# The start of a gated FNet and SwiGLU kernel: a hand-written order, a split first load, and a shorter warming on a constant

## The chip, the cores and the metric

The kernel runs on one core of a Trainium2 chip. The metric is the device time of one execution in microseconds (us). Besides the times of plain runs there is one profiled execution, whose trace gives the start and duration of every instruction.

The core's engines are named as in the profile: PE (TensorE matmuls), PEld (TensorE's weight loads, which overlap matmuls), DVE (VectorE), ACT (ScalarE), POOL (GpSimd) and SP (SyncE, which issues most DMAs). Each engine works through its own list of instructions in the order in which the program holds them, and waits on semaphores for what other engines and DMAs deliver.

## The reference

```python
x = A_x                                                  # 2048 x 512
g = sigmoid((x * gate_w).sum(-1, keepdims=True))
a = Cr @ (x @ Dr.T) - Ci @ (x @ Di.T)                    # DFT over hidden (512) and sequence (2048)
b = (silu(x @ w1) * (x @ w3)) @ w2                       # w1, w3: 512 x 1376, w2: 1376 x 512
return g * a + (1 - g) * b
```

## The kernel before

All matmuls run on float32 data in the fp32r format. Each operand is split into a high part (`high`, L107, an ACT copy that rounds to fp32r) and a low part (`low`, L110, DVE subtracts the high part from the source), and each product takes three matmuls: high by high, high by low, low by high (`mm3`, L117). In every instruction of this kind the weights are a 128 x 128 tile and the moving operand is 128 x 512.

On top of that, every product of two matrices of 2 x 2 blocks is computed with seven block products instead of eight. The operands of these products are the blocks themselves and sums of them. For x, in `OPS` (L202), the forms are B11, B21, B22 and the sums T1 to T4, with T1 = B12 - B11, T2 = B22 - T1, T3 = B22 - B12 and T4 = B21 - T2 (`SUMS`, `sum_xo`). For a chunk of the weights, the forms are three plain blocks (`WA`) and four sums (`WU`, split into `WB`).

The work has two stages.

- **gate and up** (to about 217 us). Items n = (chunk of 128 columns of w1 and w3, half of the sequence) are worked off by `gate_up(n)`. An item consists of products X (`first1`: WA block 0 by B11), Y (`first2`: WA block 1 by B21), and five more in banks X and Z: with T2, T3, T1 (weights from WB), T4 (from WA) and B22 (from WB). Each product of an item is six matmuls, and 42 make an item. `gate_up(n)` also issues X and Y of item n + 3 (`LOOK` = 3) and prepares the weights for the next item. The loads of weights (`load_w`, one 512 KB transfer for a chunk w, to the tile `ws`) and of x (`load_xo`, four blocks of 512 KB, to the tiles `xs_B`) are issued on SP; results (`store_h`) and prepared weights (`low_wb`) are stored by POOL.
- **the DFT and w2 products** (tile P, the rest of the time). The change does not touch them.

Item 0 is different: its T sums are not there yet, so `plain` computes it with eight block products, into four PSUM banks C00, C01, C10 and C11. `half(i, j, ...)` issues six matmuls into one of them. Chunk 0's block A21 and x's block B12, which only item 0 needs as they are, are split into two borrowed tiles, `a21` and `b12`.

The first lines of the program load the first 128 KB of chunk 0 and x's B11, fill a tile `warm` with zeros on DVE, and run eleven bf16 matmuls on it (`WARM`, L398), which have no part in the result. Then come the other loads, then the preparation of the first operands and the products of item 0, X and Y of items 1 to 3, the T sums, and the prepared weights of chunks 1 to 4.

What is not visible in the lines is the order in which the engines run this start. Up to L674 the program is ordered by a planner, which interleaves the instructions of the start on each engine as it estimates them to become ready. In the trace, matmuls of X1 stand between those of item 0, for example. At L674 `tc.manual_schedule()` is entered, and from there on each engine runs its instructions in the order in which the program's lines issue them. `gate_up` has hooks for such work: functions put into `early`, `mid` and `at_end` for item n are called at these points of `gate_up(n)`.

PSUM has eight banks. Item 0 uses banks 0, 4, 6 and 7; X of item n is in bank n % 4, Y in 4 + n % 2, Z in 6 + n % 2. A bank is written again only when its last reader is done.

Of the kernel before, what the change touches and what calls it, by code (L numbers as in the profile page):

```python
# [12 lines left out]
P = 128  # L13
# [8 lines left out]
NG = NST // 2  # L22
NC = (F + P - 1) // P
NP2 = (NC + 1) // 2
WARM = 11
LOOK = 3
K = 9
W2_AT = (9, 11, 13, 15)
# [4 lines left out]
def fnet_swiglu_gate_kernel(  # L33
# [46 lines left out]
    def bank(k, name):  # L80
        return psum.tile([P, 512], F32, tag=f"ps{k}", name=name)
# [31 lines left out]
    def split(hi, lo, src):  # L113
        high(hi, src)
        low(hi, lo, src)
# [89 lines left out]
    def sum_xo(g, k, t):  # L205
        ST[g, k] = t
        nc.vector.tensor_sub(t, *(ST[g, v] for v in SUMS[k]))
# [5 lines left out]
    def split_xo(g, k):  # L213
        split(*xo_parts(g, k))
# [21 lines left out]
    def prep_wa(w, lo=0, hi=3):  # L236

        if lo == 0:
            WA[w] = wap.tile([P, 2, 3, 256], F32R, tag="wa", name=f"wa{w}")
        split(*wa_parts(w, lo, hi))  # L240
# [24 lines left out]
    def prep_wb(w):  # L265
        sums_wb(w)
        high_wb(w)
        low_wb(w)
# [10 lines left out]
    G = {}  # L279

    def first1(n):
        x = bank(n % 4, f"X{n}")
        prod(x, n, 0, 0, True)
        s1 = s1p.tile([P, 512], F32, tag="s1", name=f"s1_{n}")
        nc.scalar.activation(s1, x, AF.Copy)
        G[n] = (x, s1)

    def first2(n):

        y = bank(4 + n % 2, f"Y{n}")  # L290
        prod(y, n, 1, 1, True)
        s1 = G[n][1]
        nc.vector.tensor_add(s1, s1, y)
        put_score(n, 0, s1)
# [28 lines left out]

    early, mid, at_end = {}, {}, {}

    def run(work, n):
        for f in work.get(n, ()):
# [2 lines left out]
    def gate_up(n):  # L332
        last = NI - 1
        x, s1 = G.pop(n)
        z = bank(6 + n % 2, f"Z{n}")
        if n == last - 1:

            u2, g1 = (s1p.tile([P, 512], F32, tag="s1", name=f"{k}_{n}") for k in ("u2", "g1"))
        else:
            h = hp.tile([P, 1024], F32, tag="h", name=f"h{n}")  # L340
            u2, g1 = h[:, :512], h[:, 512:]
        u4 = u4p.tile([P, 512], F32, tag="u4", name=f"u4_{n}")
        nw = WSET[n + 1] if n < last else 0
# [23 lines left out]
        nc.vector.tensor_add(u4, u4, x)  # L367
        if nw is not None:
            low_wb(nw)
        run(mid, n)  # L370
        prod(z, n, 2, 6, False, True)
        nc.vector.tensor_add(u2, u2, z)
        nc.vector.tensor_mul(u2, s1, u2)  # L373
        store_h(n, 0, u2)
        if wa is not None:
            WA[wa] = wap.tile([P, 2, 3, 256], F32R, tag="wa", name=f"wa{wa}")
# [18 lines left out]
    nc.vector.memset(warm, 0.0)  # L395
    wps = bank(7, "wps")
    for n in range(WARM):
        nc.tensor.matmul(wps, warm[:, :P], warm, start=True, stop=True)  # L398
    nc.scalar.activation(act0, warm[:, :24], AF.Silu)

    def plain(b12, a21):

        c = {}

        def half(i, j, w, x, start):
            if start:
                c[i, j] = bank((0, 4, 6, 7)[2 * i + j], f"C{i}{j}")
            for r in range(2):
                sl = slice(r * P, (r + 1) * P)
                mm3(c[i, j], w(0, sl), w(1, sl), x(r, 0), x(r, 1), start and r == 0,  # L410
                    not start and r == 1)

        def wa(k):
            return lambda h, sl: WA[0][:, h, k, sl]

        def xb(k):
            return lambda q, h: XO[0][:, h, k, q, :]

        w21 = lambda h, sl: a21[:, h, sl]
        x12 = lambda q, h: b12[:, h, q * 512 : (q + 1) * 512]  # L420
        s1 = s1p.tile([P, 512], F32, tag="s1", name="s1_0")
        g1 = u4p.tile([P, 512], F32, tag="u4", name="g1_0")
        h = hp.tile([P, 1024], F32, tag="h", name="h0")
        yield half(0, 0, wa(0), xb(0), True)
        yield half(1, 0, w21, xb(0), True)
        half(0, 0, wa(1), xb(1), False)
        nc.scalar.activation(s1, c[0, 0], AF.Silu)
        yield half(1, 0, wa(2), xb(1), False)
        nc.vector.tensor_mul(h[:, :512], s1, c[1, 0])
        store_h(0, 0, h[:, :512])  # L430
        half(0, 1, wa(0), x12, True)
        yield half(1, 1, w21, x12, True)
        half(0, 1, wa(1), xb(2), False)
        nc.scalar.activation(g1, c[0, 1], AF.Silu)
        half(1, 1, wa(2), xb(2), False)
        nc.vector.tensor_mul(h[:, 512:], g1, c[1, 1])
        yield store_h(0, 1, h[:, 512:])
# [11 lines left out]
    step = plain(b12, a21)  # L449
    prep_wa(0, 0, 1)  # L450
    for q in range(2):
        split(XO[0][:, 0, 0, q], XO[0][:, 1, 0, q], ST[0, "B11"][:, q * 512 : (q + 1) * 512])
    next(step)
    split(a21[:, 0], a21[:, 1], WS[0][:, 3])
    next(step)
    prep_wa(0, 1, 3)
    split_xo(0, "B21")
    next(step)
    split(b12[:, 0], b12[:, 1], ST[0, "B12"])
    next(step)  # L460
    split_xo(0, "B22")
    next(step)
    free(*zt)
    WS.pop(0)
    load_w(4)
    prep_wa(1)
    first1(1)
    first2(1)
    gate1(1)
    sum_xo(0, "T1", hp.tile([P, 1024], F32, tag="h", name="t1"))  # L470
    sum_xo(0, "T2", ST[0, "B11"])
    prep_wa(2)
    first1(2)
    first2(2)
    gate1(2)
    split_xo(0, "T2")
    prep_wb(1)
    sum_xo(0, "T3", ST[0, "B12"])
    split_xo(0, "T3")
    prep_wa(3)  # L480
    first1(3)
    first2(3)
    gate1(3)
    split_xo(0, "T1")
    prep_wa(4)
    sum_xo(0, "T4", ST[0, "B21"])
    split_xo(0, "T4")
    free(*(ST[0, b] for b in ("B11", "B21", "B12", "B22")))
# [506 lines left out]
```

## Time and profile before

| | us |
|---|---|
| median of 3 runs | 711.27 |
| lowest and highest run | 711.21, 711.48 |
| profiled execution, its own time | 710.88 |
| its span, first to last instruction | 709.1 |
| PE busy | 703.9 (99%), 3089 matmuls |
| DVE busy | 604.6 (85%) |
| ACT busy | 369.6 (52%) |
| POOL busy | 64.0 (9%) |

The span leaves out what lies before the first and after the last instruction, 1.8 us here. In a timeline, a row shows the start, the time to the end of the last instruction that is merged into it, the engine, the line, the operation, the tiles written and read (out<-in), the shape, the count, and in brackets how long the engine was idle ahead of it and what ended that. The tile names that matter here: `wps` is the warming matmuls' bank, `C` item 0's banks, `X`, `Y`, `Z` those of the items, `xo` the split forms of x, `wa` and `wb` the split weights, `wu` the weight sums, `ws` and `xs_B` the raw loads, and `a` and `b` the borrowed tiles for A21 and B12. A matmul's row ends 0.39 us after its start while the next one starts 0.23 us after it: matmuls are pipelined, so the distance of starts is what counts.

### The profile page before, as it was taken

To read this page: it belongs to the slowest core of one execution; us is meant where nothing else is said; L and a number is where in the kernel's file an instruction comes from. 1 tells how busy PE (TensorE), PEld (TensorE's weight loads), DVE (VectorE), ACT (ScalarE), POOL (GpSimd) and SP (SyncE) were. 2 spreads that over 40 slices of the span, in tenths; PEclk is the share of its full clock that TensorE was granted. 3 is DMA by queue.
4 is the path that set the end of the run, shared out by engine and by line. 5 is a ranking of instruction groups with operands and counts; after the bars stand their busy time and mean duration, and the time that the engine had idled before them with its cause. 6 is when DMAs were issued, how large, how long until landed. Compare 5 with 4: busy or idle time off the path is not lost.

```text
span 709.1 us, 8589 instructions
## 1 busy us (share of the span) xinstructions
PE 703.9 (99%) x3089; PEld 579.1 (82%) x3089; DVE 604.6 (85%) x733; ACT 369.6 (52%) x478; POOL 64.0 (9%) x118
## 2 busy tenths in 40 slices
PE   9999999999999999999999999999999999999997
PEld 6888888888888888888888888888888888888886
DVE  6979988787679999887999599969997896898985
ACT  6665555655446754454554553544455455455451
POOL 0011111121110000000110001100110000000000
PEclk9999999999999999999999999999999999999999
DMA  7575546589997556712596238814999971773932
GB/s 281 196 295 215 211 188 253 186 313 359 413 412 271 220 207 232 288 60 89 175 358 254 90 122 322 342 48 190 382 419 416 354 270 58 296 285 135 323 119 89
DMA packets 45403, 172.54 MB, mean 243 GB/s; under 512 B 5296, under 2 KB 5424, under 8 KB 41520
## 3 DMA queue, kind: packets, MB, share of 16 engines
q1 hardware_dynamic: 32464, 118.50, 45.2%
q0 software_dynamic: 12608, 52.97, 18.9%
q8 instruction: 24, 0.39, 0.2%
q10 hardware_dynamic: 288, 0.52, 0.2%
q14 instruction: 19, 0.16, 0.1%
HBM read 114.82 MB, written 57.16 MB: 243 GB/s over the span
## 4 chain that ended last, share of the span: by engine, by line
PE 99%; DMA 1%; DVE 0%; ACT 0%; SPq 0%; issue 0%
PE P L119 69%; PE X L119 16%; PE Z L119 8%; PE Y L119 4%; PE C L119 2%; DMA xs_B<-xt 1%; DVE xo L111 0%; DVE zc L788 0%; ACT xo L108 0%; SPq L224 0%
## 5 line engine op out<-in xcount | busy, mean ns | idle before, releaser
L119 PE MATMUL P<-zo,a 128*128 128x512 f32 x1344 | 305.5, 390 | 0.0
L119 PEld LDWEIGHTS P<-zo,a 128*128 128x128 f32 x1344 | 252.1, 188 | 53.2 <-DVE zo L111 1.2
L108 ACT ACTIVATE zo<-B 128x1024 fp32r<-128x1024 f32 (+1 forms) x182 | 189.3, 1045 | 184.5 <-PE P L119 93.2
L111 DVE TENSOR_TENSOR zo<-B,zo 128x1024 fp32r<-128x1024 f32 (+1 forms) x182 | 217.9, 1204 | 48.2 <-ACT zo L108 47.4
L119 PE MATMUL P<-zo,H 128*128 128x512 f32 x468 | 106.2, 389 | 0.0
L119 PEld LDWEIGHTS P<-zo,H 128*128 128x128 f32 x468 | 87.9, 188 | 18.2
L645 DVE TENSOR_TENSOR B<-B,B 128x1024 f32<-128x1024 f32 (+1 forms) x78 | 93.0, 1192 | 0.1
L119 PE MATMUL X<-xo,wb 128*128 128x512 f32 x378 | 92.7, 390 | 0.0
L119 PEld LDWEIGHTS X<-xo,wb 128*128 128x128 f32 x378 | 71.0, 188 | 14.7
L119 PE MATMUL P<-zo,Y 128*128 128x512 f32 x336 | 76.3, 390 | 0.0
L119 PEld LDWEIGHTS P<-zo,Y 128*128 128x128 f32 x336 | 63.1, 188 | 13.1
L322 POOL DMA_DIRECT2D hsp<-h x42 | 23.0, 547 | 126.5 <-DVE h L373 75.6
L119 PE MATMUL X<-xo,wa 128*128 128x512 f32 x126 | 32.3, 390 | 0.0
L119 PE MATMUL Z<-xo,wa 128*128 128x512 f32 x126 | 32.3, 391 | 0.0
L119 PE MATMUL Y<-xo,wa 128*128 128x512 f32 x126 | 32.1, 390 | 0.0
L119 PE MATMUL Z<-xo,wb 128*128 128x512 f32 x126 | 32.1, 390 | 0.0
L648 DVE TENSOR_TENSOR B<-B,B 128x1024 f32<-128x1024 f32 x26 | 31.7, 1219 | 0.0
L863 ACT ACTIVATE zu<-P 128x512 f32<-128x512 f32 x32 | 19.1, 598 | 20.4 <-PE P L119 20.3
L367 DVE TENSOR_TENSOR u<-u,X 128x512 f32<-128x512 f32 x21 | 14.4, 687 | 17.7 <-PE X L119 15.5
L119 PEld LDWEIGHTS Z<-xo,wa 128*128 128x128 f32 x126 | 23.6, 188 | 5.3 <-DVE xo L111 0.4
L119 PEld LDWEIGHTS Y<-xo,wa 128*128 128x128 f32 x126 | 23.7, 188 | 4.9
L119 PEld LDWEIGHTS X<-xo,wa 128*128 128x128 f32 x126 | 23.7, 188 | 4.9
(134 smaller groups left out, 551.3 us busy)
## 6 DMA issues: line engine op xcount, KB each, us to landing
B<-cc SPq DMA_DIRECT2D x64, 512.0 KB, 6.1
hsp<-h POOLq DMA_DIRECT2D x42, 256.0 KB, 3.6
B<-hsp SPq DMA_DIRECT2D x20, 512.0 KB, 9.9
wbsp<-wb POOLq DMA_DIRECT2D x8, 1024.0 KB, 4.3
wb<-wbsp SPq DMA_DIRECT2D x8, 1024.0 KB, 7.8
B<-zsp SPq DMA_DIRECT2D x16, 512.0 KB, 8.4
H<-w2sp SPq DMA_DIRECT2D x6, 1024.0 KB, 9.0
ws<-w SPq DMA_DIRECT2D x11, 512.0 KB, 6.1
```

The source lines that it names most:

```text
L108: nc.scalar.activation(hi, src, AF.Copy)
L111: nc.vector.tensor_sub(lo, src, hi.bitcast(F32))
L119: nc.tensor.matmul(ps, u, v, start=first and n == 0, stop=last and n == 2, skip_group_check=chain)
L322: nc.gpsimd.dma_start(hsp[g, b + k, j // 2, :, j % 2 * 512 : (j % 2 + 1) * 512], h)
L367: nc.vector.tensor_add(u4, u4, x)
L645: nc.vector.tensor_add(t, t, RAW[blk, b, q][:, :n])
L648: nc.vector.tensor_sub(t, RAW[blk, "B12", q], t)
L863: nc.scalar.activation(U[name][:, r], ps[r], AF.Copy)
```

## The change

- `tc.manual_schedule()` is entered before the first load instead of at L674, so the whole start runs in the order written.
- That order is new. After A11 B11 of item 0 come X1, then A21 B11 of item 0, then X2; B21 is used after these. The weights of chunks 1 and 2 are split in two steps, block A11 first. C00 to C11 are then finished, and Y1, Y2, X3 and Y3 follow.
- The loads are reordered and cut: chunks 1 and 2 are loaded in two transfers, the first 128 KB (A11) ahead of the rest, and B11 of x in two transfers of 512 columns.
- In item 0 (`half`) the three matmuls are ordered high by high, low weight by high x, high weight by low x. The other products keep their order.
- The warming reads a constant of ones that the program holds anyway, instead of the tile that DVE filled, and has nine matmuls.
- The sum T4, the low part of T1, the split of T4 and the sum of X and Y of item 2 and 3 move from the start into hooks of `gate_up(1)`; `second` is a new hook after the copy of the Z bank.

```diff
-WARM = 11
+WARM = 9
...
-        nc.sync.dma_start(ST[g, k], xt[g, XRAW.index(k)])
+        n = 512 if not g and k == "B11" else 1024
+        for i in range(0, 1024, n):
+            nc.sync.dma_start(ST[g, k][:, i : i + n], xt[g, XRAW.index(k), :, i : i + n])
...
     def first1(n):
+        copy_x(n, prod1(n))
+
+    def prod1(n):
         x = bank(n % 4, f"X{n}")
         prod(x, n, 0, 0, True)
+        return x
...
         nc.scalar.activation(u4, z, AF.Copy)
+        run(second, n)
...
+    ctx.enter_context(tc.manual_schedule())
     load_w(0, 0, 1)
     load_xo(0, "B11")
-    warm = s1p.tile([P, 1024], mybir.dt.bfloat16, tag="s1", name="warm")[:, :512]
-    nc.vector.memset(warm, 0.0)
+    warm = nc.const_aps.tensor(1.0, [P, 512], mybir.dt.bfloat16)
...
+    load_w(1, 0, 1)
     load_w(0, 1, 4)
+    load_w(2, 0, 1)
     load_xo(0, "B21")
     load_xo(0, "B12")
-    load_w(1)
+    load_w(1, 1, 4)
     load_xo(0, "B22")
-    load_w(2)
+    load_w(2, 1, 4)
     load_w(3)
...
+            for n, (u, v) in enumerate(((0, 0), (1, 0), (0, 1))):
+                nc.tensor.matmul(C[i, j], wp(u, sl), xp(r, v), start=start and r == n == 0,
+                                 stop=not start and r == 1 and n == 2)
...
+    split(*wa_parts(0, 0, 1))
     for q in range(2):
         split(XO[0][:, 0, 0, q], XO[0][:, 1, 0, q], ST[0, "B11"][:, q * 512 : (q + 1) * 512])
+    half(0, 0, 0, 0, True)
+    new_wa(1)
+    split(*wa_parts(1, 0, 1))
+    x1 = prod1(1)
     split(a21[:, 0], a21[:, 1], WS[0][:, 3])
+    half(1, 0, None, 0, True)
+    split(*wa_parts(0, 1, 3))
+    new_wa(2)
+    split(*wa_parts(2, 0, 1))
+    x2 = prod1(2)
     WS.pop(0)
     load_w(4)
+    split_xo(0, "B21")
+    half(0, 0, 1, 1, False)
+    split(b12[:, 0], b12[:, 1], ST[0, "B12"])
+    copy_x(1, x1)
+    half(1, 0, 2, 1, False)
+    split(*wa_parts(1, 1, 3))
+    half(0, 1, 0, None, True)
+    copy_x(2, x2)
+    sums_wb(1)
+    nc.scalar.activation(s1, C[0, 0], AF.Silu)
+    split_xo(0, "B22")
+    half(1, 1, None, None, True)
+    sum_xo(0, "T1", t1)
+    high(*wa_parts(2, 1, 3)[::2])
+    nc.vector.tensor_mul(h0[:, :512], s1, C[1, 0])
+    store_h(0, 0, h0[:, :512])
+    half(0, 1, 1, 2, False)
+    sum_xo(0, "T2", ST[0, "B11"])
+    low(*wa_parts(2, 1, 3))
+    half(1, 1, 2, 2, False)
+    free(*zt)
+    new_wa(3)
+    split(*wa_parts(3, 0, 3))
+    nc.scalar.activation(g1, C[0, 1], AF.Silu)
+    split_xo(0, "T2")
+    y1 = prod2(1)
+    high(*xo_parts(0, "T1")[::2])
+    nc.vector.tensor_mul(h0[:, 512:], g1, C[1, 1])
+    store_h(0, 1, h0[:, 512:])
+    y2 = prod2(2)
+    high_wb(1)
+    sum_g(1, y1)
+    first1(3)
+    sum_xo(0, "T3", ST[0, "B12"])
+    y3 = prod2(3)
+    low_wb(1)
+    split_xo(0, "T3")
     gate1(1)
+    new_wa(4)
+    split(*wa_parts(4, 0, 3))
...
+    do(early, 1, sum_xo, 0, "T4", ST[0, "B21"])
+    do(early, 1, lambda: low(*xo_parts(0, "T1")))
+    do(second, 1, lambda: split_xo(0, "T4"))
+    do(second, 1, free, *(ST[0, b] for b in ("B11", "B21", "B12", "B22")))
+    do(second, 1, sum_g, 2, y2)
+    for n, at, y in ((2, 1, None), (3, 1, y3)):
+        if y is not None:
+            do(mid, at, sum_g, n, y)
+        do(mid, at, gate1, n)
...
-    ctx.enter_context(tc.manual_schedule())
     for n in range(1, NI):
         gate_up(n)
```

More of the change, by code (lines that the diff above doesn't have):

```diff
@@ L234, in wa_parts, with new_wa @@
         return (*(flat(WA[w][:, h, lo:hi]) for h in range(2)), flat(WS[w][:, lo:hi]))
[L236 to L240, printed above, removed]
+    def new_wa(w):
+        WA[w] = wap.tile([P, 2, 3, 256], F32R, tag="wa", name=f"wa{w}")
     WU = {}
@@ L263, in low_wb @@
             nc.gpsimd.dma_start(wbsp[w], WB[w].bitcast(F32))
[L265 to L268, printed above, removed]
     def prod(ps, n, wi, xi, start, chain=False):
@@ L281, in first1, with copy_x @@
     def first1(n):
+        copy_x(n, prod1(n))
+    def prod1(n):
         x = bank(n % 4, f"X{n}")
         prod(x, n, 0, 0, True)
+        return x
+    def copy_x(n, x):
         s1 = s1p.tile([P, 512], F32, tag="s1", name=f"s1_{n}")
@@ L288, in first2, with prod2, sum_g @@
     def first2(n):
+        sum_g(n, prod2(n))
+    def prod2(n):
         y = bank(4 + n % 2, f"Y{n}")
         prod(y, n, 1, 1, True)
+        return y
+    def sum_g(n, y):
         s1 = G[n][1]
@@ L322, in store_h @@
         nc.gpsimd.dma_start(hsp[g, b + k, j // 2, :, j % 2 * 512 : (j % 2 + 1) * 512], h)
-    early, mid, at_end = {}, {}, {}
+    early, second, mid, at_end = {}, {}, {}, {}
     def run(work, n):
@@ L375, in gate_up @@
         if wa is not None:
-            WA[wa] = wap.tile([P, 2, 3, 256], F32R, tag="wa", name=f"wa{wa}")
+            new_wa(wa)
             parts_a = wa_parts(wa, 0, 3)
@@ L399, in fnet_swiglu_gate_kernel @@
     nc.scalar.activation(act0, warm[:, :24], AF.Silu)
[L401 to L437, printed above, removed]
+    load_w(1, 0, 1)
     load_w(0, 1, 4)
+    load_w(2, 0, 1)
     load_xo(0, "B21")
     load_xo(0, "B12")
-    load_w(1)
+    load_w(1, 1, 4)
     load_xo(0, "B22")
-    load_w(2)
+    load_w(2, 1, 4)
     load_w(3)
@@ L448, in fnet_swiglu_gate_kernel, with half @@
     b12, a21 = zt[0].rearrange("p h a n -> p h (a n)"), zt[1][:, :, 0]
-    step = plain(b12, a21)
-    prep_wa(0, 0, 1)
+    C = {(i, j): bank((0, 4, 6, 7)[2 * i + j], f"C{i}{j}") for i in range(2) for j in range(2)}
+    def half(i, j, w, x, start):
+        wp = lambda h, sl: a21[:, h, sl] if w is None else WA[0][:, h, w, sl]
+        xp = lambda q, h: b12[:, h, q * 512 : (q + 1) * 512] if x is None else XO[0][:, h, x, q, :]
+        for r in range(2):
+            sl = slice(r * P, (r + 1) * P)
+            for n, (u, v) in enumerate(((0, 0), (1, 0), (0, 1))):
+                nc.tensor.matmul(C[i, j], wp(u, sl), xp(r, v), start=start and r == n == 0,
+                                 stop=not start and r == 1 and n == 2)
@@ L451, in fnet_swiglu_gate_kernel @@
+    s1 = s1p.tile([P, 512], F32, tag="s1", name="s1_0")
+    g1 = u4p.tile([P, 512], F32, tag="u4", name="g1_0")
+    h0 = hp.tile([P, 1024], F32, tag="h", name="h0")
+    t1 = hp.tile([P, 1024], F32, tag="h", name="t1")
+    new_wa(0)
+    split(*wa_parts(0, 0, 1))
     for q in range(2):
         split(XO[0][:, 0, 0, q], XO[0][:, 1, 0, q], ST[0, "B11"][:, q * 512 : (q + 1) * 512])
-    next(step)
+    half(0, 0, 0, 0, True)
+    new_wa(1)
+    split(*wa_parts(1, 0, 1))
+    x1 = prod1(1)
     split(a21[:, 0], a21[:, 1], WS[0][:, 3])
-    next(step)
@@ L456, in fnet_swiglu_gate_kernel @@
[L456 to L463, printed above, removed]
+    half(1, 0, None, 0, True)
[3 more added lines that the diff above has]
+    x2 = prod1(2)
     WS.pop(0)
     load_w(4)
-    prep_wa(1)
-    first1(1)
-    first2(1)
-    gate1(1)
-    sum_xo(0, "T1", hp.tile([P, 1024], F32, tag="h", name="t1"))
-    sum_xo(0, "T2", ST[0, "B11"])
-    prep_wa(2)
@@ L473, in fnet_swiglu_gate_kernel @@
[L473 to L488, printed above, removed]
+    split_xo(0, "B21")
[3 more added lines that the diff above has]
+    half(1, 0, 2, 1, False)
```

## The prediction

> **What bounds the kernel now.** I read the page first, then PE's waits, then the timelines of PE, ACT and DVE for the first 45 us, because the diff touches nothing that runs later.
>
> The page's head and its chain of waits:
>
> ```profile
> span 709.1 us, 8589 instructions
> ...
> PE 99%; DMA 1%; DVE 0%; ACT 0%; SPq 0%; issue 0%
> PE P L119 69%; PE X L119 16%; PE Z L119 8%; PE Y L119 4%; PE C L119 2%; DMA xs_B<-xt 1%; DVE xo L111 0%; DVE zc L788 0%; ACT xo L108 0%; SPq L224 0%
> ```
>
> The end is set by one stream of matmuls, preceded by the load of the first x block. The change keeps all 3078 real matmuls (3089 less 11 warming ones). Only two things can move the end: when the stream begins, and how often it stops. The timeline of PE (start, us, operation, count):
>
> ```profile
> 1.19 4.67 PE L398 MATMUL wps<-warm 128*128 128x512 bf16 x11 [1.19 <-DVE warm L395]
> 5.62 0.50 PE L119 MATMUL C<-xo,wa 128*128 128x512 f32 x1
> 6.35 1.43 PE L119 MATMUL C<-xo,wa 128*128 128x512 f32 x5 [0.22 <-DVE xo L111]
> 7.62 1.53 PE L119 MATMUL C<-xo,a 128*128 128x512 f32 x6
> 8.98 3.15 PE L119 MATMUL C<-xo,wa 128*128 128x512 f32 x12
> 11.96 1.52 PE L119 MATMUL C<-b,wa 128*128 128x512 f32 x6
> ...
> 31.00 1.83 PE L119 MATMUL Z<-xo,wa 128*128 128x512 f32 x6
> 32.67 1.53 PE L119 MATMUL Y<-xo,wa 128*128 128x512 f32 x6
> ```
>
> A product of six starts 1.36 us after the one before it (7.62 to 8.98), 0.227 a matmul. Against that the stream stops three times: the first six take 2.00 (5.62 to 7.62), 0.64 too many; the twelve from 8.98 take 2.98 instead of 2.72, 0.26 too many (the low part of B21); the Z product takes 1.67, 0.31 too many (T4). Together 1.21. At the later starts of an item (35.39, 44.91, and so on to 73.47) the step is 9.52 for 42 matmuls: nothing is lost.
>
> What feeds the stream, in ACT's timeline and then DVE's:
>
> ```profile
> 4.94 1.15 ACT L108 ACTIVATE xo<-xs_B 128x512 fp32r<-128x512 f32 x2 [1.31 <-DMA xs_B<-xt]
> 7.19 1.06 ACT L108 ACTIVATE xo<-xs_B 128x1024 fp32r<-128x1024 f32 x1 [0.27 <-DMA xs_B<-xt]
> 8.46 1.06 ACT L108 ACTIVATE b<-xs_B 128x1024 fp32r<-128x1024 f32 x1 [0.21 <-DMA xs_B<-xt]
> ```
>
> ```profile
> 8.29 1.23 DVE L111 TENSOR_TENSOR xo<-xs_B,xo 128x1024 fp32r<-128x1024 f32 x1 [0.45 <-ACT xo L108]
> ...
> 30.12 1.23 DVE L111 TENSOR_TENSOR xo<-xs_B,xo 128x1024 fp32r<-128x1024 f32 x1 [0.17 <-ACT xo L108]
> ...
> 33.15 1.23 DVE L111 TENSOR_TENSOR wb<-wu,wb 128x1024 fp32r<-128x1024 f32 x1 [0.53 <-ACT wb L108]
> ...
> 36.22 0.95 DVE L111 TENSOR_TENSOR wa<-ws,wa 128x768 fp32r<-128x768 f32 x1
> ...
> 41.50 0.69 DVE L367 TENSOR_TENSOR u<-u,X 128x512 f32<-128x512 f32 x1 [2.26 <-ACT wb L108]
> ```
>
> Loads land 1.27 us apart per 512 KB. DVE is nearly full from 8.29 until it first has 2.26 to spare, at 41.5. That is the second limit: a PE that starts earlier runs into DVE.
>
> **The start.** The memset (0.27 us on DVE) goes; ACT and SP start work at 0.73, so PE can begin near 0.75. Nine matmuls at the 0.427 pitch of the warming rows end near 4.6, before the data, so the warming itself costs nothing. The first half of B11 is issued at 1.19 as before. Its second half, 256 KB at 1.27 per 512, is 0.64 behind it, so it lands about 4.92 - 0.64 = 4.28 (bounds: 3.69, if it took the 2.5 us of the 128 KB load; 4.92, if it landed with the whole; I take 4.3, because the landings' even spacing carries it). From there ACT needs 0.63 and PE 0.05: first matmul at 4.98 instead of 5.62, a gain of **0.64**. The Trainium skill, "DMA: Bandwidth & Descriptors", anatomy of one DMA, gives about 2.0 us plus bytes over 436 GB/s: that half would land at 3.8, and the start would gain some 0.4 more; the 512 KB row (3.73 where that rule gives 3.2) speaks for the later value.
>
> **The first six.** The new order puts both matmuls that need only high x first, so two run before the low part (DVE 4.96 to 5.64), and the second half lands at 5.0 as the whole did. With the first two at 0.427 the next product starts at 6.62: 1.64 for six, 0.28 lost instead of 0.64.
>
> **The next loads.** Two more 128 KB pieces now precede B21, at 0.32 to 0.4 each: B21 lands near 8.0, not 7.17, B12 near 9.2. What hides it: the products X1, C10, X2 on B11 alone keep PE from 6.62 to 10.70, and B21's low part is ready at 10.3. The 0.26 stop goes; without this cover it would be about 0.5. SP's wait for w4 stands on w0's last reader, at 7.9 as before, with only w5's load behind it. POOL stores h0 later (near 17 and 21 instead of 13.25 and 19.59); h1's buffer is needed at 26, and a store took 2.5.
>
> **The written order further on.** I walked ACT and DVE in their new order with row durations, one DVE operation freeing the engine after 1.14 (1024 columns), 0.87 (768), 0.60 (512), 0.34 (256), ACT after 0.94 to 0.52. PE goes from 6.62 through twelve products (16.3 us) to the end of X3 at 22.94. Three waits appear:
> - T3. Its high part now queues on ACT behind X3's copy (23.14), so it runs 23.66 to 24.72 and DVE's low part to 25.98. The T3 product starts at 25.66, its second matmul would follow at 25.89: 0.15, plus 0.11 because the first matmul after a wait is followed after 0.33 instead of 0.23 (6.35 to 6.68 in the trace). **0.26.**
> - T1. Its low part stands behind w4's (26.00) and T4's sum (26.87): 28.01 to 29.23. The T1 product starts at 28.63 and wants it at 28.86: 0.42 plus 0.11. **0.53.** T4's low part, ready at 30.43, is then no wait: the 0.31 goes.
> - w5. DVE goes on with T4 low (1.14), a sum (0.60), four weight sums (1.47) and one add (0.60), waits for wb2's high part until 33.6, then wb2 low (1.14), two sums, add and multiply (2.5) and w5's low part, ready at 38.2; in the trace before, at 37.17. X5 starts at 37.32 and wants it at 37.78: about 0.5 plus 0.11. **0.61.**
>
> After that DVE has the slack seen at 41.5, and nothing changes. Below zero these waits cannot go; at the upper end each could be 0.3 longer.
>
> **Sum.** Gains 0.64 + 1.21 = 1.85; losses 0.28 + 0.26 + 0.53 + 0.61 = 1.68; net 0.17 faster. Against the profiled execution, 710.88 (span 709.1 and 1.8 around it), that is 710.7; the median of the runs is 0.39 above that execution, so I predict **711.1**.
>
> **Rivals.**
> 1. DVE keeps up: the three waits (1.40) do not come, for instance because operations hand on earlier than their rows end. 711.27 - 0.17 - 1.40 = 709.7. For it: the old stop at T4 shows DVE late by only 0.3. Against: DVE's row durations leave no room, and three idle stretches (before B21, B22 and T3, 2.3 us together) are new. 0.13.
> 2. The clock, slower. Warming runs at 0.427 a matmul up to 5.43, the stream at 0.24 from 6.68; nine matmuls are 0.8 us less activity, with a pause before the data. If the slow pitch lasts on, each microsecond of it costs 1 - 0.227/0.427 = 0.47. From 0.4 us longer the gain is gone; 3.4 us longer costs 1.6, 711.1 + 1.6 = 712.7. Against: pause and stops together are under 0.7 us. The granted clock in the rows reads 1.00 even while warming, so it cannot decide. 0.10. The Trainium skill, "TensorE: Matmul & The Clock Gate", Part 1, says the clock is halved until a busy window of about 3.4 us, free-running, has passed; by it a missed window is this rival, and the pitches agree with half and full rate.
> 3. The split brings nothing: both halves land at 4.9. The start's 0.6 is lost, 711.7, within measurement. 0.10.
>
> **How the numbers follow.** A measurement of this kernel tells about 0.2%, 1.42 us, from no change. The forecast (0.67) and rival 3 lie inside: same 0.77. Rival 1 is faster by 1.57: 0.13. Rival 2 at its full price is slower by just over 1.4: 0.10. The forecast's own range is 710.4 to 712.0 (start 0.4 either way, waits up to 0.3 longer each); to hold 8 in 10 it reaches to rival 1's 709.7 and most of rival 2: 709.7 to 712.3.
>
> **What would show it.** Right: first C matmul near 5.0, X1 near 6.6, no stop at B21, and PE waits on DVE at the T3, T1 and w5 products. Wrong: X5 following without a gap (rival 1), C matmuls at 0.43 beyond 6.5 (rival 2), a first C matmul at 5.6 (rival 3), or a moved end while item 6 still starts near 73.3: something after the start that I hold untouched.

## The result and the profile after

| | before | after |
|---|---|---|
| median, us | 711.22 (14 runs) | 712.70 (14 runs) |
| lowest and highest | 710.83, 711.51 | 712.17, 713.89 |
| profiled execution, us | 710.88 | 712.88 |
| its span, us | 709.1 | 711.1 |

The ratio is 1.002, 95% interval 1.0013 to 1.0028: the change makes the kernel about 1.5 us slower, or 0.2%. That is small, but the interval leaves out 1. 711.1 was predicted, with 712.3 as the upper end.

The page's head and its chain of waits, after:

```profile
span 711.1 us, 8595 instructions
PE 95%; DVE 2%; DMA 1%; ACT 1%; issue 0%; SPq 0%
PE P L119 69%; PE X L119 15%; PE Z L119 7%; PE Y L119 4%; PE C L434 1%; DMA xs_B<-xt 1%; DVE xo L111 1%; ACT xo L108 0%; DVE s L300 0%; DVE wa L111 0%; SPq L226 0%; DVE xs_B L209 0%; ACT wb L108 0%; SPq L202 0%; ACT wa L108 0%
```

PE's share of the chain falls from 99% to 95%. The difference is not the time lost; it shows what the stream of matmuls now waits for. The chain runs through SyncE's issues up to 3.54, then through the load of B21 (3.54 to 10.40; before, it was the load of B11, 1.19 to 4.92), and from 25 to 40 us for the most part through DVE and ACT. PE's timeline after (start, us, operation, count; brackets: idle time and what ended it) shows where it stops:

```profile
0.78 4.00 PE L409 MATMUL wps<-const-bfloat16-1.0 128*128 128x512 bf16 x9 [0.78 <-PEq L1003]
5.38 1.93 PE L434 MATMUL C<-xo,wa 128*128 128x512 f32 x6 [0.60 <-ACT xo L108]
7.14 1.54 PE L119 MATMUL X<-xo,wa 128*128 128x512 f32 x6
8.65 1.91 PE L434 MATMUL C<-xo,a 128*128 128x512 f32 x6
10.40 1.54 PE L119 MATMUL X<-xo,wa 128*128 128x512 f32 x6
11.78 0.61 PE L434 MATMUL C<-xo,wa 128*128 128x512 f32 x2
12.79 2.58 PE L434 MATMUL C<-xo,wa 128*128 128x512 f32 x10 [0.40 <-DVE xo L111]
15.21 1.52 PE L434 MATMUL C<-b,wa 128*128 128x512 f32 x6
...
27.45 1.76 PE L119 MATMUL Z<-xo,wb 128*128 128x512 f32 x6
29.05 1.55 PE L119 MATMUL X<-xo,wa 128*128 128x512 f32 x6
30.44 0.39 PE L119 MATMUL X<-xo,wb 128*128 128x512 f32 x1
31.05 1.43 PE L119 MATMUL X<-xo,wb 128*128 128x512 f32 x5 [0.22 <-DVE xo L111]
32.31 1.52 PE L119 MATMUL Z<-xo,wa 128*128 128x512 f32 x6
...
39.16 0.73 PE L119 MATMUL X<-xo,wa 128*128 128x512 f32 x2
40.07 1.20 PE L119 MATMUL X<-xo,wa 128*128 128x512 f32 x4 [0.18 <-DVE wa L111]
41.11 1.54 PE L119 MATMUL X<-xo,wb 128*128 128x512 f32 x6
```

Each distance of starts, less 1.36 for every six matmuls, is a loss. Beside what the prediction gave for it:

| place | working | us lost | predicted |
|---|---|---|---|
| first C matmul | at 5.38 (5.62 before) | gain 0.24 | gain 0.64 |
| first six | 7.14 - 5.38 - 1.36 | 0.40 | 0.28 |
| X1 and A21 B11 | 10.40 - 7.14 - 2.72 | 0.54 | 0 |
| X2 | 11.78 - 10.40 - 1.36 | 0.02 | 0 |
| products on B21 | 15.21 - 11.78 - 2.72 | 0.71 | 0 |
| T3 | 29.05 - 27.45 - 1.36 | 0.24 | 0.26 |
| T1 | 32.31 - 30.44 - 1.36 | 0.51 | 0.53 |
| w5 | 41.11 - 39.16 - 1.36 | 0.59 | 0.61 |

The losses come to 3.01 against 1.68 predicted. With the old stops gone (1.21, as predicted), the stream is 3.01 - 0.24 - 1.21 = 1.56 later than before. Direct readings agree: item 3's products start at 46.57 instead of 44.91 (1.66 later; the other 0.10 are steps of 1.38 or 1.39 where 1.36 is counted), the last matmul 1.68 later. Next to nothing is lost in between.

The remaining 0.3 of the profiled executions' 2.0 lies behind the last store. It landed at 709.84, and the span ends 1.27 later; before, 708.15 and 0.97. In the trace's records SyncE closes the program with waits on the semaphores of the transfers, 0.06 us apart. Before, two of them come after that landing; after, seven. This goes with the number of transfers in the program, in all fourteen profiles of this case: 0.97 to 0.98 with 329 (the kernel before), 0.91 to 0.92 with 330, 1.35 with 331, 1.27 to 1.28 with 332 (the kernel after).

ACT's timeline after shows what the first two unpredicted stops waited for; DVE's shows the rows whose ends (27.74, 31.00 and 40.02) end the stops at T3, T1 and w5:

```profile
4.69 1.33 ACT L108 ACTIVATE xo<-xs_B 128x512 fp32r<-128x512 f32 x2 [1.16 <-DMA xs_B<-xt]
8.18 0.42 ACT L108 ACTIVATE a<-ws 128x256 fp32r<-128x256 f32 x1 [1.85 <-DMA ws<-w]
10.42 1.06 ACT L108 ACTIVATE xo<-xs_B 128x1024 fp32r<-128x1024 f32 x1 [0.86 <-DMA xs_B<-xt]
```

```profile
26.51 1.23 DVE L111 TENSOR_TENSOR xo<-xs_B,xo 128x1024 fp32r<-128x1024 f32 x1 [0.33 <-ACT xo L108]
...
29.78 1.22 DVE L111 TENSOR_TENSOR xo<-t,xo 128x1024 fp32r<-128x1024 f32 x1
...
39.07 0.95 DVE L111 TENSOR_TENSOR wa<-ws,wa 128x768 fp32r<-128x768 f32 x1
```

ACT stands idle for 1.85 us until A21 is there, and for 0.86 until B21 is. The second half of B11 landed at 5.37, the rest of chunk 0 at 8.16 (5.88 before), B21 at 10.40 (7.17 before) and B12 at 11.69 (8.44 before). The windows view of both kernels shows the lower traffic behind it, in its last two columns (share of the DMA engines, GB/s; ahead of them length, busy time of PE, PEld, DVE, ACT, POOL, and PE's clock). First before, then after:

```profile
3.00:5.00 2.00, 2.00 (x6) 0.64 (x5) 0.43 (x1) 0.48 (x2) 0.00 (x0) 1.00 1.01 381
5.00:7.00 2.00, 1.78 (x7) 0.88 (x6) 1.40 (x3) 1.92 (x4) 0.00 (x0) 1.00 1.02 408
```

```profile
3.00:5.00 2.00, 1.78 (x5) 0.31 (x3) 0.43 (x1) 0.72 (x2) 0.00 (x0) 1.00 0.80 259
5.00:7.00 2.00, 1.62 (x6) 0.98 (x7) 1.64 (x3) 1.26 (x3) 0.00 (x0) 1.00 0.73 226
```

With the loads cut and reordered, the traffic is 259 GB/s from 3 to 5 us and 226 from 5 to 7, instead of 381 and 408. Over those 4 us that is 0.97 MB instead of 1.58, or 0.6 of it. The prediction had taken the spacing of before, 1.27 us per 512 KB, for every byte. This is no accident of one execution: from 3 to 5 us four other profiles with the loads of before read 371 to 389 GB/s, and two others with the loads of after 251 and 267.

One part of B21's lateness is when it is issued. SyncE issues one transfer after another, 0.47 us apart, and B21 is now the seventh instead of the fourth. First before, then after (two issues in a row, B21's and B12's):

```profile
2.12 0.91 SPq L200 DMA_DIRECT2D xs_B<-xt  x2
```

```profile
3.54 0.91 SPq L202 DMA_DIRECT2D xs_B<-xt  x2
```

So of the 3.23 us by which B21 lands later, 1.42 are its later issue, and 1.81 a longer way from issue to landing (6.86 instead of 5.05). No run tests the issue by itself.

### The profile page after: what moved, and what is told of

The parts are those of the page before. It is cut to its first block, busy times and chain, and to the rows that moved or that the text cites. A ratio compares the mean times of both kernels' runs of the same rounds, so it can differ in the third digit from the quotient of the medians.

```text
span 711.1 us, 8595 instructions
## 1 busy us (share of the span) xinstructions
PE 704.9 (99%) x3087; PEld 577.9 (81%) x3087; DVE 604.9 (85%) x734; ACT 369.3 (52%) x480; POOL 64.2 (9%) x118
## 4 chain that ended last, share of the span: by engine, by line
PE 95%; DVE 2%; DMA 1%; ACT 1%; issue 0%; SPq 0%
PE P L119 69%; PE X L119 15%; PE Z L119 7%; PE Y L119 4%; PE C L434 1%; DMA xs_B<-xt 1%; DVE xo L111 1%; ACT xo L108 0%; DVE s L300 0%; DVE wa L111 0%; SPq L226 0%; DVE xs_B L209 0%; ACT wb L108 0%; SPq L202 0%; ACT wa L108 0%
## 5 line engine op out<-in xcount | busy, mean ns | idle before, releaser
L119 PEld LDWEIGHTS Z<-xo,wb 128*128 128x128 f32 x126 | 23.6, 188 | 5.2 <-DVE xo L111 0.4
```

Source lines behind the costliest of these rows:

```text
L119: nc.tensor.matmul(ps, u, v, start=first and n == 0, stop=last and n == 2, skip_group_check=chain)
```

## The experiments

Three causes were set against each other for the lateness. **P**: the two 128 KB pieces of chunks 1 and 2, issued ahead of B21, cost more than their bytes. **H**: the halving of B11 does. **C**: nine warming matmuls leave too long a pause, and PE starts at its slow pitch in some executions. The expected stops at T3, T1 and w5 were tested besides.

**B11 in one transfer again** (from the kernel after):

```diff
-        n = 512 if not g and k == "B11" else 1024
+        n = 1024
```

> The changed kernel, but with x's B11 in one transfer; the two early 128 KB pieces of chunks 1 and 2 stay. In the changed kernel the rest of chunk 0 landed at 8.16 us and B21 at 10.40, where I had counted on 6.3 and 8.0. Theory P (the early 128 KB pieces starve the DMA engines): the rest of chunk 0 still lands after 7.5, B21 near 10, the kernel stays within 0.5 us of the changed one, near 712.7. Theory H (halving B11 does it): the rest of chunk 0 lands near 6.3, B21 near 8.0, the first product starts at 5.65, the stops before A21 and B21 go, and the kernel gains about 1.0 us, 711.7.

Measured: 713.73 (712.16 to 715.61), ratio 1.0032 [1.002, 1.0044]. PE's timeline:

```profile
6.39 2.93 PE L434 MATMUL C<-xo,wa 128*128 128x512 f32 x6 [1.62 <-ACT xo L108]
9.12 1.67 PE L119 MATMUL X<-xo,wa 128*128 128x512 f32 x6
```

Two things at once. B11 landed at 5.69, so PE paused 1.62 us after warming, and then the first six took 2.73 instead of 1.36: a matmul every 0.43 us up to 9.12, and every 0.23 from 9.47. That is C, seen in a trace; it was rival 2. The Trainium skill, "TensorE: Matmul & The Clock Gate", Part 1, puts such a start at half rate down to a busy window of about 3.4 us that has to be filled; the slow pitch lasted 2.7 to 3.1 us from 6.39 on, somewhat less. And B21 landed at 8.91, later than the 7.17 to 7.68 of the five profiles in which only B11 whole and chunk 0 go ahead of it, with 273 GB/s from 3 to 5 us: the halving is not all of the lateness.

**Chunks 1 and 2 whole, at the place of their first pieces** (from after):

```diff
-    load_w(1, 0, 1)
+    load_w(1)
     load_w(0, 1, 4)
-    load_w(2, 0, 1)
+    load_w(2)
...
-    load_w(1, 1, 4)
...
-    load_w(2, 1, 4)
```

> The changed kernel, but chunks 1 and 2 are each loaded whole (512 KB) where only their first 128 KB stood, so 768 KB more go ahead of B21, and no 128 KB piece is left behind B11. Theory P: the DMA engines stay full; by 1.27 us per 512 KB the rest of chunk 0 lands near 7.6 and B21 near 10.1, so B21 is not later than in the changed kernel although far more bytes precede it, and the time is 712.2 to 712.7. Theory H: the engines still starve, B21 lands near 10.4 + 1.9 = 12.3, and the kernel loses nearly 2 us more, 714.5.

Measured: 713.27 (712.44 to 715.17), ratio 1.0028 [1.0018, 1.0037]. B21 landed at 10.66. That is 0.26 later than in the kernel after, with 768 KB more ahead of it; at 1.27 us per 512 KB those bytes would be 1.9. So the lateness is not one of bytes: the same number of transfers stands ahead of B21 as in the kernel after, two of them four times as long, and it lands hardly later. The time, outside the 712.2 to 712.7 that P gave, is no better, since X1 now waits for the whole of chunk 1 (0.38 us of idle time).

**The two pieces issued on ACT's queue** (from after):

```diff
-    load_w(1, 0, 1)
+    load_w(1, 0, 1, nc.scalar)
+    load_w(2, 0, 1, nc.scalar)
     load_w(0, 1, 4)
-    load_w(2, 0, 1)
```

> The changed kernel, but the two 128 KB pieces of chunks 1 and 2 are issued on ACT's queue, just ahead of ACT's first split, instead of on SP's. If the hole in the DMA traffic comes from short transfers standing between the others in one queue, the engines stay full: the rest of chunk 0 lands near 6.3, B21 near 8.0, and the kernel gains about 1.2 us on the changed one, 711.4. If it comes from the number and size of the pieces whatever their queue (theory P in its plain form), the rest of chunk 0 lands after 7.5 and B21 near 10, and the time stays near 712.7.

Measured: 712.78 (712.14 to 713.91), ratio 1.0018 [1.0008, 1.0028]. The median stands for neither kind of its runs: five lie at 712.1 to 712.3 and five at 713.3 to 713.9. The profile, 712.25, is of the first kind. In it B21 landed at 8.61 instead of 10.40, and the stops at A21 and B21 are gone; but the halves of B11 landed at 5.08 and 6.00, and the first C matmul came at 5.79. So in this profile part of what was won at 8 to 15 us was lost at 5. PE pauses 1.26 us behind the warming there; whether the slower five are C, no trace shows.

**Eleven warming matmuls** (from after):

```diff
-WARM = 9
+WARM = 11
```

> The changed kernel with 11 warming matmuls on the constant instead of 9. They end near 5.5, just after the first product could start (5.38), so the start itself loses 0.1 at most. Theory P+H (the loss comes from the loads): the median stays near 712.7 and B21 still lands after 10. Theory C (nine matmuls leave the slow pitch on in many executions, at 0.47 us for each us): the spread of the runs, 712.2 to 713.9 in the changed kernel, shrinks to that of the kernel before (0.7 us), and the median falls by 0.5 or more, to 712.2 or less.

Measured: 712.32 (711.96 to 712.82), ratio 1.0016 [1.0007, 1.0026]. The median is 0.38 lower, and the spread of ten runs 0.86 us instead of the 1.72 of after's fourteen. Theory C had asked for 712.2 or less, so it is met in the spread and just missed in the median. The two intervals overlap, and the 0.38 is a reading, not a proof; but nine of these ten runs are below the median of after. In the one profile of after the slow pitch was gone when the data came (the first two C matmuls follow each other at 0.33, and from 6.44 at 0.23), so a cost of the pitch would belong to other executions, of which there is no trace. A rival is not excluded: the same loads land at different times, B21 at 10.40, 10.06 and 9.50 in the profiles of after, of this run and of the two moves below.

**The warming alone** (from before):

```diff
-WARM = 11
+WARM = 9
...
-    warm = s1p.tile([P, 1024], mybir.dt.bfloat16, tag="s1", name="warm")[:, :512]
-    nc.vector.memset(warm, 0.0)
+    warm = nc.const_aps.tensor(1.0, [P, 512], mybir.dt.bfloat16)
```

> The kernel before, with nothing changed but the warming: nine matmuls on the constant, from 0.78 to 4.6, and then a pause of 1 us until the first product at 5.62. Theory C: the pitch of the first products stays at 0.43 for longer than in the kernel before, and the median is 0.4 to 1.6 us above it, 711.8 to 713. Theory P+H: the loads are untouched, so the time is that of before, 711.3 within 0.2.

Measured: 711.41 (710.96 to 713.69), ratio 1.0008 [0.9998, 1.0017]. Its median can't be told from before, but four of its ten runs lie at 711.99 or above, against one of the 31 runs of before beside them (in another batch it was four of 31). Its profile, 711.44, doesn't show C: after a pause of 1.38 us, 0.24 less than with B11 in one transfer above, the first six take 2.00 us (6.16 to 8.16), as before. With the loads of before, B11 landed in it at 5.46, not 4.92: the landing of the same load varies by half a microsecond from one execution to the next.

**The split of B11 alone** (from before):

```diff
-        nc.sync.dma_start(ST[g, k], xt[g, XRAW.index(k)])
+        n = 512 if not g and k == "B11" else 1024
+        for i in range(0, 1024, n):
+            nc.sync.dma_start(ST[g, k][:, i : i + n], xt[g, XRAW.index(k), :, i : i + n])
```

> The kernel before, with nothing changed but x's B11 in two transfers. Theory P: no starving; the first C product starts near 5.3 instead of 5.62, but B21 lands at 7.2 to 7.4 as before and the twelve matmuls on B21 wait for it, so the time is within 0.3 us of before, 711.2. Theory H: the rest of chunk 0 and B21 land 1 us or more later, and the kernel is slower by 0.7 us or more.

Measured: 712.65 (711.86 to 713.14), ratio 1.0014 [1.0005, 1.0024]. One cut, nothing else, and 1.3 us are lost against the 711.36 of before beside it. PE's timeline, ACT's, and the windows view:

```profile
5.50 2.30 PE L119 MATMUL C<-xo,wa 128*128 128x512 f32 x6
7.64 1.55 PE L119 MATMUL C<-xo,a 128*128 128x512 f32 x6
9.70 0.73 PE L119 MATMUL C<-xo,wa 128*128 128x512 f32 x2 [0.51 <-ACT xo L108]
10.96 2.56 PE L119 MATMUL C<-xo,wa 128*128 128x512 f32 x10 [0.53 <-DVE xo L111]
```

```profile
7.04 0.42 ACT L108 ACTIVATE a<-ws 128x256 fp32r<-128x256 f32 x1 [1.05 <-DMA ws<-w]
8.59 1.06 ACT L108 ACTIVATE xo<-xs_B 128x1024 fp32r<-128x1024 f32 x1 [0.61 <-DMA xs_B<-xt]
```

```profile
3.00:5.00 2.00, 2.00 (x6) 0.63 (x5) 0.46 (x2) 1.04 (x2) 0.00 (x0) 1.00 1.02 286
5.00:7.00 2.00, 2.00 (x7) 1.39 (x6) 1.35 (x2) 0.63 (x1) 0.00 (x0) 1.00 0.83 312
```

The first half landed at 4.28, exactly where the prediction had it (eleven warming matmuls keep PE until 5.50 here), but the second at 5.33 and B21, issued 0.47 later than before, at 8.57 instead of 7.17. The traffic falls to 286 and 312 GB/s. The products on B21, which in the order of before come right behind the first two, stop twice, with 0.51 and 0.53 us of idle time.

**B11 cut by partitions instead of columns** (from before; two transfers of 64 partitions, so each row stays 4 KB):

```diff
-        nc.sync.dma_start(ST[g, k], xt[g, XRAW.index(k)])
+        n = 64 if not g and k == "B11" else 128
+        for i in range(0, 128, n):
+            nc.sync.dma_start(ST[g, k][i : i + n], xt[g, XRAW.index(k), i : i + n])
```

> The kernel before, with x's B11 in two transfers as in e5, but cut by partitions (64 and 64) instead of columns, so that the rows, and with them the packets, stay 4 KB. In e5 the packets were 2 KB, B21 landed at 8.57 instead of 7.17, and the kernel lost 1.3 us. If short packets are the cause, this one loses nothing: B21 lands near 7.2, 711.3. If one more transfer in the first microseconds is the cause, it loses as much as e5: B21 near 8.5, 712.6.

Measured: 712.58 (711.62 to 712.99), ratio 1.0012 [1.0002, 1.0022]. Halves at 4.94 and 6.08, B21 at 8.81, 280 and 310 GB/s. The same fall of the traffic with rows of full length: the shorter rows are not its cause. The time is lost elsewhere than with columns, though: ACT's first copy of B11 needs both of these halves, so the first C matmul came at 6.85. And four of the ten runs, at 711.6 to 711.7, lose only 0.4.

**B12 in two transfers** (from before):

```diff
-        nc.sync.dma_start(ST[g, k], xt[g, XRAW.index(k)])
+        n = 512 if not g and k == "B12" else 1024
+        for i in range(0, 1024, n):
+            nc.sync.dma_start(ST[g, k][:, i : i + n], xt[g, XRAW.index(k), :, i : i + n])
```

> The kernel before, with x's B12 (the fourth load, 8.44) in two transfers of 512 columns instead of B11 (the second). If an extra short transfer costs whenever it comes, B12 and all behind it land 0.5 us or more later, and the time is 711.5 to 712.2. If it costs only while the queue has no backlog, in the first microseconds, nothing lands later than in the kernel before by more than 0.2, and the time is 711.2.

Measured: 711.22 (710.82 to 711.85), ratio 1.0 [0.9991, 1.0009]. The same cut, three places later in the list of loads, costs no time: 374 GB/s from 3 to 5 us. It does lower the traffic when B12's turn comes, to 368 GB/s from 5 to 7 us and 373 from 7 to 9 (408 and 424 before), and chunk 1 lands 2.90 us behind B21 instead of 2.55. But that is a tenth of the traffic and not a quarter, and no matmul waits for these loads. So of the two answers that were set against each other neither is quite right: an additional transfer costs traffic in both places, more among the very first ones, and time only there.

**Two moves against the stops at T3 and T1** (from after):

```diff
-    first1(3)
+    x3 = prod1(3)
     sum_xo(0, "T3", ST[0, "B12"])
+    high(*xo_parts(0, "T3")[::2])
+    copy_x(3, x3)
     y3 = prod2(3)
     low_wb(1)
-    split_xo(0, "T3")
+    low(*xo_parts(0, "T3"))
     gate1(1)
+    sum_xo(0, "T4", ST[0, "B21"])
     new_wa(4)
...
-    do(early, 1, sum_xo, 0, "T4", ST[0, "B21"])
```

> The changed kernel with two lines moved: T3's high part goes ahead of X3's copy on ACT, and the sum T4 ahead of the split of w4 on DVE; the loads are as in the changed kernel. If the waits at T3 (0.24), T1 (0.49) and w5 (0.57) come, as I worked out, from ACT's and DVE's order, the first two vanish, a wait of 0.3 to 0.4 for w4's low part comes in at X4, the one at w5 stays near 0.5, and the stream is 0.4 us earlier at the end: 712.3. If DVE's amount of work in this stretch sets them whatever the order, the sum of the waits stays at 1.3 and so does the time, 712.7.

Measured: 712.20 (711.60 to 713.12), ratio 1.0015 [1.0006, 1.0024]. PE's timeline:

```profile
27.93 1.83 PE L119 MATMUL X<-xo,wa 128*128 128x512 f32 x6
29.59 1.54 PE L119 MATMUL X<-xo,wb 128*128 128x512 f32 x6
30.97 1.55 PE L119 MATMUL Z<-xo,wa 128*128 128x512 f32 x6
...
38.84 1.20 PE L119 MATMUL X<-xo,wa 128*128 128x512 f32 x4 [0.18 <-DVE wa L111]
```

The T1 product takes 1.38 (29.59 to 30.97) and T3's stop is gone, but X4 now takes 1.66, 0.30 too many, for w4's low part, which stands behind T4's sum; w5's stop stays. The three stops cost 0.90 together with X4's, 0.44 less than after, and the median moves by 0.50, with overlapping intervals: the first two stops are indeed ACT's and DVE's order, as the walk had it. The profile is that of its fastest run, 711.60; the same loads as after land earlier in it, B21 at 9.50, and A21 and B21 cost 0.27 instead of 1.25.

**B21 and T4 split in halves, in the order of before** (from before, with item 0's matmuls in the order of after):

```diff
-                mm3(c[i, j], w(0, sl), w(1, sl), x(r, 0), x(r, 1), start and r == 0,
-                    not start and r == 1)
+                for n, (u, v) in enumerate(((0, 0), (1, 0), (0, 1))):
+                    nc.tensor.matmul(c[i, j], w(u, sl), x(r, v), start=start and r == n == 0,
+                                     stop=not start and r == 1 and n == 2)
...
-    split_xo(0, "B21")
+    split_halves(0, "B21")
...
-    split_xo(0, "T4")
+    split_halves(0, "T4")
```

(`split_halves` calls `split` for each half of 512 columns.)

> The kernel before with its loads, its warming and its planner left alone; only the splits of B21 and of T4 are done in two halves of 512 columns each, and item 0's matmuls in the order high by high, low weight by high x, high weight by low x. If the stops of the kernel before at the low parts of B21 (0.26) and T4 (0.31) and part of the first product's (0.2) are waits for the second half of a long DVE operation, they go, the stream is 0.5 to 0.7 us earlier at the end and the time 710.6 to 710.8. If DVE's amount of work sets them, the stops only move, and the time is that of before, 711.2 within 0.2.

Measured: 711.51 (711.44 to 711.88), ratio 1.0005 [0.9996, 1.0014]: the hoped-for gain isn't there. PE's timeline:

```profile
28.92 1.21 PE L119 MATMUL X<-xo,wa 128*128 128x512 f32 x4 [0.32 <-DVE wa L111]
32.07 1.42 PE L119 MATMUL Z<-xo,wa 128*128 128x512 f32 x5 [0.23 <-DVE xo L111]
```

At the start the stream runs without the stop at B21, and then it stops for w4 (0.62, 27.99 to 29.97) and T4 (0.60, 31.36 to 33.32). PE came earlier to a DVE that had the same amount of work, in two instructions more: the stops moved and grew.

**All undone but the order** (from after: eleven warming matmuls, B11 whole, the pieces on ACT's queue, and the two moves):

```diff
-WARM = 9
+WARM = 11
...
-        n = 512 if not g and k == "B11" else 1024
+        n = 1024
...
-    load_w(1, 0, 1)
+    load_w(1, 0, 1, nc.scalar)
+    load_w(2, 0, 1, nc.scalar)
     load_w(0, 1, 4)
-    load_w(2, 0, 1)
...
-    first1(3)
+    x3 = prod1(3)
...
```

> The changed kernel's written order with every suspected cost taken out at once: B11 in one transfer, the two 128 KB pieces on ACT's queue, eleven warming matmuls, and the two moves that took away the waits at T3 and T1. If loads, warming and these waits are all of the loss, it is back at the kernel before within 0.4 us: 711.0 to 711.6, with B21 landing at 8.0 to 8.6 and only the wait at w5 left. If the written order costs something more, it stays at 712 or above.

Measured: 712.29 (712.18 to 712.36), ratio 1.0015 [1.0005, 1.0024]: missed, by some 0.7 at least. B11 landed at 5.54 beside the pieces of the other queue (at 3.72 and 5.94), and the first C matmul came at 6.25. B21 landed at 8.45, although it was issued at 2.13, as before: the later issue is not all of its lateness. And 0.38 us of the miss lie behind the last store, where this program of 331 transfers takes 1.35 instead of 0.97. Moving the pieces to another queue does not undo them, as the run with ACT's queue had shown already. So one more, in which the loads really are those of before:

**The written order with the loads of before** (from after, with eleven warming matmuls; chunks 1 and 2 are loaded whole behind B12 and B22, and the first block of both is taken from chunk 0's tile instead, so that X1 and X2 work on other data):

```diff
-WARM = 9
+WARM = 11
...
-        n = 512 if not g and k == "B11" else 1024
+        n = 1024
...
-    load_w(1, 0, 1)
     load_w(0, 1, 4)
-    load_w(2, 0, 1)
...
-    load_w(1, 1, 4)
+    load_w(1)
...
-    load_w(2, 1, 4)
+    load_w(2)
...
-    split(*wa_parts(1, 0, 1))
+    split(*wa_parts(1, 0, 1)[:2], flat(WS[0][:, :1]))
...
-    split(*wa_parts(2, 0, 1))
+    split(*wa_parts(2, 0, 1)[:2], flat(WS[0][:, :1]))
```

> The changed kernel's written order and eleven warming matmuls, with the loads of the kernel before, transfer for transfer (B11 whole, chunks 1 and 2 whole behind B12 and B22). So that X1 and X2 can still run early, the first block of chunks 1 and 2 is taken from chunk 0's, which is already there: the values of these products are not the reference's, the work is. If the loads are what made the changed kernel slow, B21 lands near 7.2, there is no stop before A21 and B21, the three waits at T3, T1 and w5 stay (1.3 us in all), the stream is 0.5 us later at the end than in the kernel before, and the time is 711.6 to 711.9, 0.5 under the changed kernel with eleven warming matmuls (712.3). If the written order itself makes the loss, the time stays at 712.2 or above.

Measured: 711.79 (711.40 to 711.93 and one of 714.49), ratio 1.0007 [0.9998, 1.0016]. PE's timeline:

```profile
6.00 1.93 PE L432 MATMUL C<-xo,wa 128*128 128x512 f32 x6 [0.37 <-ACT xo L108]
7.77 1.55 PE L119 MATMUL X<-xo,wa 128*128 128x512 f32 x6
9.15 1.53 PE L432 MATMUL C<-xo,a 128*128 128x512 f32 x6
10.53 1.52 PE L119 MATMUL X<-xo,wa 128*128 128x512 f32 x6
...
29.85 0.39 PE L119 MATMUL X<-xo,wb 128*128 128x512 f32 x1
30.44 1.43 PE L119 MATMUL X<-xo,wb 128*128 128x512 f32 x5 [0.20 <-DVE xo L111]
```

The traffic is back at 371 and 403 GB/s from 3 to 5 and from 5 to 7 us, B21 lands at 7.52, and 9.15 and 10.53 follow each other in steps of 1.38: no stop at A21, and the starts run on without one at B21 either. The stops at T1 (29.85 to 30.44), T3 and w5 remain. All runs but one are below every run of the kernel after.

Of the three causes, P and H both hold, and C in part: with the two pieces alone the traffic from 3 to 5 us falls to 273 GB/s, with the halving alone to 286, and the slow pitch is seen in one profile.

So the time goes, by medians: 711.25 before; 711.79 with the new order on the old loads (+0.54); 712.32 with the cut and reordered loads (+0.53, of which 0.30 are the closing waits); 712.70 with nine warming matmuls instead of eleven (+0.38). The intervals of neighbouring steps overlap, so no step is shown by its time alone; the whole, 1.5, is. The first step is in the prediction's own sum: without the start's gain of 0.64, the losses of 1.68 outweigh the old stops of 1.21 by 0.47. So the new order pays only through the earlier start. None of the kernels was faster than the one before.

## Why the prediction was wrong, step by step

Between the forecast of 710.7 for the profiled execution and the measured 712.88 lie 2.2 us. The landings of A21 and B21 are 1.25 of them, the start 0.40, the closing waits 0.31, the first six 0.12; the rest is small.

- **The written order further on: right.** The three waits were worked out at 0.26, 0.53 and 0.61, and measured 0.24, 0.51 and 0.59. The walk through ACT's and DVE's queues with row durations held to 0.02, although PE reached these products 1.8 us later than the walk had it; ACT and DVE are about as late in this stretch (T3's high part at 25.43 instead of 23.66), so the distances stayed. Rival 1 is out: DVE does not keep up.
- **The start: the term was mis-sized.** The first half was to land at 4.3 and landed at 4.67; the first C matmul came at 5.38, not 4.98, a gain of 0.24 instead of 0.64. 4.28 was measured with the split alone, so the half itself is worth what was worked out in one execution, and not in another. The rule of the Trainium skill ("DMA: Bandwidth & Descriptors", anatomy of one DMA), by which it would have landed at 3.8, is given there for one DMA on GpSimd's path, while SyncE issues this one behind another load; the first halves of all seven profiles with B11 cut landed at 4.25 to 5.08, further from 3.8 than from 4.3.
- **The first six: mis-sized by 0.12.** The third matmul started 0.72 after the first, for the low part, about as worked out (the two ahead of it came 0.33 apart and not 0.427, which this wait hides). But the one behind it followed after 0.34 (6.10 to 6.44): the 0.11 that come with each wait, which the prediction counted at T3, T1 and w5, and not here. The weight loads show the wait:

```profile
6.10 0.53 PEld L434 LDWEIGHTS C<-xo,wa 128*128 128x128 f32 x3 [0.43 <-DVE xo L111]
```

That the second half landed at 5.37, not 5.0, has no part in it: with the loads of before and B11 whole, the first six of the written order lose 0.41 (6.00 to 7.77).

- **The next loads: this step failed.** The two pieces were priced at their bytes, and the halving at nothing: the even spacing of the landings was taken to hold for the new list too. B21 was to land near 8.0 and landed at 10.40, the rest of chunk 0 at 8.16. The cover that was named (X1, C10, X2) was there, and it hid most of the 3.2 us by which B21 came later; but chunk 0's rest carries A21, which the second of these covering products needs, and its landing was not worked out in the text. Cost: 0.54 and 0.71. What the runs showed in its place: each additional transfer puts off the issue of those behind it by 0.47, and the traffic falls (from 381 and 408 GB/s to 286 and 312 with the halving alone, to 259 and 226 with all of it). The even spacing of before held for the list of before, not as a rate that can be applied to any list.
- **The end: a term that was put at nothing.** What follows the last matmul was taken as untouched, and took 0.31 more: the closing waits, by the number of transfers.
- **The warming "costs nothing": so in this profile, perhaps not in the median.** Rival 2 was given 0.10 at its full price of 1.6; the one profile that shows it (B11 in one transfer again) lost 1.37 in the first six alone, of which some 0.4 are lost without it too. At the median its part may be some 0.4, by the run with eleven; that the slow pitch outlasts the pause in some executions of the kernel after is inferred from their spread, not seen. That its time, 712.7, is the measured one is chance: the profile of after loses nothing to the pitch and 1.25 to the landings of A21 and B21.
- **Rival 3, the split brings nothing,** named the right edit, and was still too kind: it let the halves land with the whole, and didn't let them delay what follows. No rival had that.

What stays open: why an additional transfer lowers the traffic. In the kernel after the DMA engines are busy for 0.80 and 0.73 of these stretches, so some stood without work, but with the split alone they read 1.02 from 3 to 5 us and move 286 GB/s, so there packets took longer. None of the runs tells what makes them do so.

## What to carry to other kernels

Cutting the first load to start sooner is not free at the head of a queue: here it delayed everything behind it by more than the start gained, so price the issue and the landing of every load that follows, not only that of the piece. Products that are to cover a late load must themselves be followed to their own loads. A walk through the queues of ACT and DVE with durations of the trace was good to a few hundredths of a microsecond here; where PE is made to come earlier, an engine that is nearly full can give the gain back as new stops. When a gain of tenths is at stake, what follows the last store belongs into the sum too.

## What the runs showed of the hardware

- One additional transfer among the first three (B11 in two, 256 KB each) lowers the traffic from 3 to 5 us from 381 to 286 GB/s and lands B21 at 8.57, where five profiles with B11 whole have 7.17 to 7.68; this holds whether it is cut by columns (2 KB rows) or by partitions (4 KB rows: 280 GB/s, 8.81). The same cut at the fifth load lowers the traffic by a tenth (408 to 368 GB/s from 5 to 7 us) and changes nothing in the time (711.22 and 711.25).
- SyncE issues these loads 0.47 us apart, so an additional transfer also puts off the issue of each one behind it by that much (B21's: 2.12 before, 2.59 with the split alone, 3.54 after).
- A piece on another engine's queue is no way round: with the two 128 KB pieces on ACT's queue the halves of B11 landed at 5.08 and 6.00, against 4.25 to 4.75 and 5.16 to 5.45 in the four profiles in which the pieces, or the whole chunks in their place, follow on SyncE's.
- After the last store has landed, the program's closing waits take 0.91 to 1.35 us, by the number of transfers in it (329 to 332).
- The granted clock in the rows is 1.00 both while matmuls follow each other at 0.43 us and at 0.23, so the pitch of the starts has to be read for it. In the kernel after the nine warming matmuls still follow each other at 0.42 at their end (4.14), and the pitch is the fast one when the data comes, after a pause of 0.60; in the run with a pause of 1.62 us the slow pitch lasted until 9.12.
